# A load of batch 3's keys is issued ahead of a GpSimd wait in tile 1 of a pooled-attention and SiLU kernel

## The chip, the cores and the metric

The kernel runs on one core of a Trainium2 chip. The metric is the device time of one launch in microseconds (us); less is better. The core's engines are named as the profile names them: PE (TensorE, matrix products; PEld is its weight load), DVE (VectorE), ACT (ScalarE), POOL (GpSimd) and SP (SyncE, which here only issues DMAs). Each engine works through its own list of instructions in program order, and waits at an instruction until what that needs is there. A DMA is issued by an engine and then moves its data while that engine goes on.

## The reference

Attention with pooled keys and values, and behind it a two-layer network with SiLU:

```python
def _attn_ref(q, k, v):                       # q, k, v: 8 batches, 8 heads, 576 rows, 64 columns
    k_p = k.reshape(B, H, Sp, pool, D).mean(axis=3)     # pool = 8, so Sp = 72 keys are left
    v_p = v.reshape(B, H, Sp, pool, D).mean(axis=3)
    scores = scale * np.matmul(q, k_p.transpose(0, 1, 3, 2))
    scores = scores - np.max(scores, axis=-1, keepdims=True)
    attn = np.exp(scores)
    attn = attn / (np.sum(attn, axis=-1, keepdims=True) + 1e-09)
    return np.matmul(attn, v_p)

def _moe_ref(x, w_in, w_out):                 # x: 4608 x 512, w_in: 512 x 2048, w_out: 2048 x 512
    h = x @ w_in
    g = h * (1.0 / (1.0 + np.exp(-h)))
    return g @ w_out
```

The 8 batches of 576 rows, heads side by side, are the 4608 rows of x. All inputs and the output are float32.

## The kernel before

**Tiles and batches.** The 4608 tokens are done in nine tiles of 512 (the loop over `t`, `NT` = 9). A tile computes its two products with the weights, and beside them prepares the attention of the next tile, `a = t + 1`. As a batch has 576 tokens, tile `a` needs the pooled keys and values of batches up to `a`. So tile 1 finishes the keys of batch 2 and fetches those of batch 3, tile 2 finishes those of batch 3, and so on.

**The products.** Each product is done on blocks with seven multiplications instead of eight, which needs sums of blocks beforehand: of the weights (`weight_sum` L828 and `unit_weight_sum`, into w_sum and w_sum1), of x (`unit_x_sum` L715, into x_sum) and of the hidden layer (`hidden_sum` L817, into h_sum), all on DVE. The matrix products of the first layer are L874 (banks u_psA, u_psE, u_psB), those of the second L893 (o_psA, o_psE, o_psB). DVE's L908, L925 and L903 add or copy between these banks.

**Order.** A tile's products are a string of short names (`ORDER`, `FOUR`, for tile 1 `ONE`) which is walked step by step. All other work of the tile is a list of fillers: `at(s, fn, ...)` puts a call at step `s`. `spread` (L662) sorts them by step, keeps the order in which they were given within one step, and calls each when the products have come to its step. This sets the order of every engine's list of instructions by hand; the engines then wait for one another's results. Two fillers are there only for a wait: `behind_weight_sums` (L721) and `behind_x_sums` (L718) copy one element of the last weight sum, or the last x sum, into `gate` on POOL, so that what POOL has behind it starts only after DVE's sums.

**The keys of batch 3 and later.** `load_one` (L182, its DMA for keys is L189) loads the first four of each eight rows that are pooled, 576 KB, into a tile of its own tag. `load_rest` (its DMA is L221) loads the other four and adds them onto the first, in the DMA itself; it has to wait until the first has landed. `pool_k` adds up the four that are left on POOL (`pool_rows`, L227 and L230, into kp). `k_transpose` turns kp on PE (L292, at step 34 of the tile, into kT_ps) and copies it on ACT (L298, into kz); `spread_keys` (L279, at step 35, on DVE) makes kzr of it. The values of batch 3 go by `load_one` and `load_rest` too, in two DMAs each (`load_v_half`, L211). Batch 2's keys are loaded in another way, in slots, and summed by `slot_sums` (L346) on POOL; batch 2's values have the second half added by `load_v_half(2, 1)` and are summed by `pool_rows` on DVE at step 69 of tile 1.

**POOL's list at the start of tile 1.** The last filler of tile 0 on POOL is a `spread_keys` (L279). Then come, all at step 0, `behind_weight_sums` and the `slot_sums` of batch 2's keys (five sums and results in two groups); at step 1 the adding load of batch 2's values (two DMAs); at step 3 `load_one` for batch 3's keys, then for its values; at step 5 `load_rest` for both; at step 33 the load of batch 3's queries. In tile 2 POOL goes on with `behind_x_sums`, `pool_k` and `load_one` for batch 4's keys.

Of the kernel before, what the change touches and what calls it, by code (L numbers as in the profile page):

```python
# [36 lines left out]
def kernel(  # L37
# [156 lines left out]
    def last_rows(bs):  # L194

        lasts[bs] = mid.tile([128, 2, 2 * PH], FP32, tag="r_raw", bufs=1, name="r_raw")
        return lasts[bs][:, : len(bs)]
# [28 lines left out]
    def pool_rows(dst, raw, eng=nc.gpsimd):  # L226
        eng.tensor_add(  # L227
            out=raw[:, :, : 2 * D], in0=raw[:, :, : 2 * D], in1=raw[:, :, 2 * D :]
        )
        eng.tensor_add(out=dst, in0=raw[:, :, :D], in1=raw[:, :, D : 2 * D])  # L230
# [4 lines left out]
    def value_tile(b):  # L235
        vp = mid.tile([128, 4, D], BF16, tag="vp", name="vp")
        batches[b]["vp"] = vp
        return vp
# [927 lines left out]
    for t in range(NT):  # L1166
        a = t + 1
        if t == 0:
            f = []

            def at(s, fn, *args, **kw):
                f.append((s, lambda: fn(*args, **kw)))

            for n in (0, 2, 1, 3):
                at(0, unit_x_sum, 0, n)
            for y, y_at in ((2, 0), (3, 18), (1, 66)):
                for n in range(4):
                    at(y_at + n, unit_weight_sum, y, y + 1, n)
            for n in range(3):
                at((39, 42, 43)[n], slot_sums, "k", 0, levels=(n,))  # L1180
            at(45, slot_sums, "k", 1)
            for a in range(2):
                at(50, q_transpose, 1, a, 0, QI - UT)
            for j in range(2):
                at(55, select_k, 1, j)
            at(55, copy_k, 1, slice(0, 2), nc.scalar.copy)
            for i0, i1 in ((0, SA), (SA, SLOTS), (SLOTS, SLOTS + 1)):
                at(47, load_slots, nc.gpsimd, 2, "k", i0, i1)
            at(47, load_q, 2)
            for a in range(2):  # L1190
                at(55 + a, q_transpose, 1, a, QI - UT, UT)
            at(52, attn_tables)
            for i in range(PW):
                at(63 + i, weight_sum, 0, i)
            for n in (1, 2, 3):
                at(89, weight_sum, n, 0)
            at(93, weight_sum, 1, 1)
            for j in range(2):
                at(75 + j, slot_sums, "v", j)
                at(90, select_v, 1, j)  # L1200
            at(90, copy_v, 1, 0, nc.scalar.copy, H)
            at(92, turn_v, 1)
            at(84, load_first_values, 2)
            at(48, lambda: nc.gpsimd.memset(last_rows((1, 2))[:, :, :1], 0.0))
            at(80, load_v_last, 1, 2)
            at(84, spread_keys, 1, nc.gpsimd)
            at(60, scores_half, 1, 0)
            at(73, scores_half, 1, 1)
            for n in range(2):
                at(83, denominators, 1, n)  # L1210
                at(83, reciprocals, 1, n)
            at(95, numerators, 1, 0)
            at(95, numerators, 1, 1)
            for n in range(2):
                at(95, x_half, 1, n)
            at(96, moe_tables)
            tile_products(0, FIRST, f)
            continue

        order = ORDER.get(t, FOUR if t < NT - 1 else BARE)  # L1220
        if t == NT - 1:
            order = order.replace("P4 Q4", "R4 S4")
        o = 0
        f = []

        def at(s, fn, *args, **kw):
            f.append((s, lambda: fn(*args, **kw)))

        def late(s, fn, *args, **kw):
            at(s + o, fn, *args, **kw)  # L1230

        if t == 1:
            for n in (0, 2, 1, 3):
                at(0, unit_x_sum, 1, n)
            for n in (2, 3):
                at(0, weight_sum, n, 1)
            at(0, behind_weight_sums)
        late(43, hidden_sum, 2, 0, 4)
        late(53, hidden_sum, 2, 4, 8)
        late(64 if t < NT - 1 else 57, hidden_sum, 0, 0, 4)  # L1240
        late(64 if t < NT - 1 else 62, hidden_sum, 1, 0, 4)
        late(65, hidden_sum, 0, 4, 8)
        late(66, hidden_sum, 1, 4, 8)
        late(76, hidden_sum, 3, 0, 8)
        if a < B:
            if t == 1:
                for j in range(2):
                    at(0, slot_sums, "k", j, eng=nc.gpsimd)
                    at(46, select_k, 2, j)
                    at(47, copy_k, 2, j, nc.scalar.copy)  # L1250
                at(1, load_v_half, 2, 1)
                at(69, lambda: pool_rows(value_tile(2), batches[2]["v_raw"], nc.vector))
                at(50, spread_keys, 2)
                for n in "kv":
                    at(3, load_one, 3, n)
                at(44, last_sums, 1, 2, eng=nc.vector, levels=(0,))
                at(84, last_sums, 1, 2, eng=nc.vector, levels=(1, 2))
                at(46, load_v_last, 3)
                at(86, last_values, 1, 2, eng=nc.vector)
                for n in "kv":  # L1260
                    at(5, load_rest, 3, n)
                at(33, load_q, 3)
            else:
                at(0, behind_x_sums)
                at(0, pool_k, a)
                if a + 1 < B:
                    at(0, load_one, a + 1, "k")
                at(1, pool_v, a)
                if a + 1 < B:
                    at(1, load_one, a + 1, "v")  # L1270
                    at(1, load_v_last, a + 1)
                    at(3, load_rest, a + 1, "k")
                    at(4, load_rest, a + 1, "v")
                    at(33, load_q, a + 1)
                at(34, k_transpose, a)
                at(35, spread_keys, a)
        if t < NT - 1:
            tail = QI - UT + 2 * t
            for n in range(2):
                at((22, 32)[n], q_transpose, a, n, 0, tail)  # L1280
                if tail < UT:
                    at((47, 55)[n], q_transpose, a, n, tail, UT)
            late(63, attn_tables)
            late(63, scores, a)
            late(88, sums_and_values, a)
            late(89, x_part, a, 0)
            late(89, moe_tables)
            late(95, x_part, a, 1)
        if t < NT - 1:
            for n in (0, 2, 1, 3):  # L1290
                late(102 if (t, n) == (1, 0) else 105, unit_x_sum, t + 1, n)
        tile_products(t, order, f, last=t == NT - 1)
# [28 lines left out]
```

## Time and profile before

| | |
|---|---|
| median of 3 runs | 267.33 us (267.11 to 267.76) |
| profiled execution, its own time | 269.37 us |
| its span, first to last instruction | 267.7 us |
| mean granted PE clock | 1.000 |
| busy time PE / PEld | 260.7 us (97%) / 211.8 us (79%) |
| busy time DVE / ACT / POOL | 210.2 us (79%) / 182.3 us (68%) / 116.7 us (44%) |
| chain that ended last | PE 78%, DMA 11%, POOL 5%, DVE 4% |
| DMA raw<-in_k_dram in that chain | 8% |
| first layer's products of tiles 1, 2, 3 begin on PE | 47.19, 74.69, 103.76 us |

Busy time is the time in which an engine had an instruction under way; a busy PE is not PE at its peak. The chain is followed back from the last instruction, at each step to what released it. In a timeline each line is a start in us, a length in us, engine, line of the kernel, operation, what it writes and reads, shapes and how many; in brackets stands how long the engine was idle before it and what ended that. DMA share is the mean busy share of the core's 16 DMA engines; it can go a little over 1. A DMA's time to landing is counted from its issue.

### The profile page before, as it was taken

The page shows a single profiled execution, that of the slowest core. Times are in us where ns is not written, and L with a number is a line of the kernel's source. Part 1 is how long each engine was busy: PE and PEld are TensorE (multiplying, and loading weights), DVE is VectorE, ACT ScalarE, POOL GpSimd, SP SyncE. Part 2 cuts the span into 40 slices and gives each one's busy share as a digit, 9 for nine tenths or more (in the row PEclk, how much of TensorE's full clock was granted, in tenths as well). Part 3 has the DMA queues.
Part 4 walks back from the last instruction along what each step waited for, and adds up shares of the span by engine and source line. Part 5 has one row for each costly group of instructions (what it writes and reads, how often), then busy time and mean ns, then how long its engine had stood idle before and what let it go on. Part 6 is the DMA issues. An engine that isn't in the chain of part 4 may idle for free.

```text
span 267.7 us, 7702 instructions
## 1 busy us (share of the span) xinstructions
PE 260.7 (97%) x3136; PEld 211.8 (79%) x3136; DVE 210.2 (79%) x375; ACT 182.3 (68%) x319; POOL 116.7 (44%) x156
## 2 busy tenths in 40 slices
PE   8999999999997999999999999999999999999994
PEld 4468644888886788888888888888888887888883
DVE  3878879889886959895979598859886987687862
ACT  1489867888657865886587658765876677667700
POOL 8664774590609843853296229764900000000000
PEclk9999999999999999999999999999999999999999
DMA  7999999679598799679566956699400150015004
GB/s 191 283 205 272 223 283 290 176 167 195 123 177 209 193 162 190 152 178 175 121 164 153 191 113 151 154 169 140 117 2 0 40 119 3 2 32 127 2 0 157
DMA packets 31266, 38.84 MB, mean 145 GB/s; under 512 B 9776, under 2 KB 21488, under 8 KB 31232
## 3 DMA queue, kind: packets, MB, share of 16 engines
q0 software_dynamic: 22416, 25.84, 51.9%
q1 hardware_dynamic: 8384, 11.87, 16.5%
q10 hardware_dynamic: 432, 0.66, 1.1%
q8 instruction: 24, 0.39, 0.6%
q14 instruction: 10, 0.08, 0.1%
HBM read 37.75 MB, written 9.44 MB: 176 GB/s over the span
## 4 chain that ended last, share of the span: by engine, by line
PE 78%; DMA 11%; POOL 5%; DVE 4%; issue 1%; ACT 0%; POOLq 0%; DVEq 0%
PE o_psB L893 14%; PE u_psB L874 14%; PE o_psA L893 9%; PE o_psE L893 9%; PE u_psE L874 9%; PE u_psA L874 9%; DMA raw<-in_k_dram 8%; PE o_ps L792 4%; DMA raw<-in_v_dram 3%; PE hp_ps L764 3%; POOL raw L346 2%; PE sc_ps L555 1%; PE den_ps L584 1%; PE nu_ps L609 1%; POOL raw L227 1%; DVE raw L346 1%
## 5 line engine op out<-in xcount | busy, mean ns | idle before, releaser
L874 PEld LDWEIGHTS <-w_sum 128*128 128x128 bf16 x544 | 52.9, 98 | 6.9 <-issue 0.3
L893 PEld LDWEIGHTS <-h_sum 128*128 128x128 bf16 x512 | 48.9, 98 | 7.6 <-issue 0.4
L874 PEld LDWEIGHTS <-w_in_sb 128*128 128x128 bf16 x408 | 39.8, 98 | 4.9
L893 PEld LDWEIGHTS <-h_T 128*128 128x128 bf16 x384 | 37.0, 98 | 5.2 <-issue 0.4
L874 PE MATMUL u_psA<-xT,w_in_sb 128*128 128x256 bf16 x272 | 40.7, 273 | 0.0
L874 PE MATMUL u_psB<-x_sum,w_sum 128*128 128x256 bf16 x272 | 40.2, 273 | 0.1
L893 PE MATMUL o_psA<-w_out_sb,h_T 128*128 128x256 bf16 x256 | 32.0, 273 | 0.0
L893 PE MATMUL o_psB<-w_sum,h_sum 128*128 128x256 bf16 x256 | 31.8, 273 | 0.0
L908 DVE TENSOR_TENSOR u_psE<-u_psB,p 128x512 f32<-128x512 f32 x34 | 23.6, 697 | 9.1 <-PE u_psB L874 4.7
L912 ACT ACTIVATE h_T<-u_psE 128x512 bf16<-128x512 f32 x34 | 20.3, 597 | 10.6 <-PE u_psE L874 10.3
L925 DVE TENSOR_TENSOR c<-u_psB,p 128x512 f32<-128x512 f32 x34 | 23.2, 681 | 3.1 <-PE u_psB L874 2.1
L650 DVE TENSOR_TENSOR xT<-nu_ps,rec 128x512 bf16<-128x512 f32 x28 | 17.9, 682 | 9.4 <-ACT rec L634 9.4
L903 DVE COPY u_psB<-u_psA 128x512 f32<-128x512 f32 x30 | 20.9, 698 | 4.7 <-PE u_psA L874 4.2
L912 ACT ACTIVATE h_T<-u_psB 128x512 bf16<-128x512 f32 x34 | 20.4, 600 | 5.5 <-PE u_psB L874 5.5
L912 ACT ACTIVATE h_T<-u_psA 128x512 bf16<-128x512 f32 x34 | 20.4, 601 | 5.0 <-PE u_psA L874 5.0
L906 ACT COPY p<-u_psE 128x512 f32<-128x512 f32 x34 | 20.1, 596 | 4.0 <-PE u_psE L874 4.0
L211 POOL DMA_DIRECT2D v_raw<-in_v_dram x20 | 18.0, 992 | 11.0 <-DMA v_raw<-in_v_dram 11.0
L817 DVE TENSOR_TENSOR h_sum<-h_T 128x1024 bf16<-128x1024 bf16 x32 | 21.9, 687 | 0.2 <-ACT h_T L912 0.2
L912 ACT ACTIVATE h_T<-c 128x512 bf16<-128x512 f32 x34 | 21.7, 638 | 0.1
L817 DVE TENSOR_TENSOR h_sum<-h_T,h_sum 128x1024 bf16<-128x1024 bf16 (+1 forms) x24 | 20.7, 863 | 0.2
L874 PE MATMUL u_psB<-xT,w_sum 128*128 128x256 bf16 x136 | 20.4, 273 | 0.0
L874 PE MATMUL u_psE<-x_sum,w_in_sb 128*128 128x256 bf16 x136 | 20.4, 273 | 0.0
(127 smaller groups left out, 462.0 us busy)
## 6 DMA issues: line engine op xcount, KB each, us to landing
out_dram<-o_sb SPq DMA_DIRECT2D x128, 64.0 KB
raw<-in_k_dram POOLq DMA_DIRECT2D x10, 576.0 KB, 8.7
v_raw<-in_v_dram POOLq DMA_DIRECT2D x20, 256.0 KB, 6.0
q_bf<-in_q_dram POOLq DMA_DIRECT2D x5, 576.0 KB, 9.1
w_in_sb<-in_moe_w_in_dram POOLq DMA_DIRECT2D x8, 256.0 KB, 7.6
w_out_sb<-in_moe_w_out_dram POOLq DMA_DIRECT2D x8, 256.0 KB, 8.6
r_raw<-in_v_dram SPq DMA_DIRECT2D x28, 64.0 KB
raw<-in_v_dram POOLq DMA_DIRECT2D x2, 768.0 KB, 7.9
```

The lines of the kernel that those rows point to most:

```text
L211: nc.gpsimd.dma_start(out=batches[b]["v_raw"][KM * g : KM * (g + 1)], in_=source(b, "v")[:KM, 4 * g : 4 * (g + 1), PH * half : PH * (half ...
L346: eng.tensor_add(out=dst if w == D else raw[..., :w], in0=raw[..., :w], in1=raw[..., w : 2 * w],)
L650: nc.vector.tensor_mul(out=xT[:, 2 * g : 2 * g + 2, x_cols(t, f)], in0=st["nu"][g][f], in1=inv[:, f : f + 1, :].broadcast_to([128, 2, NQ]),)
L792: nc.tensor.matmul(ps["m", m], lhsT=h_T[:, g, m * 128 : (m + 1) * 128], rhs=w_out_sb[:, g, :], start=(g == 0), stop=(g == KG - 1),)
L817: nc.vector.tensor_tensor(out=h_sum[n][:, k0:k1, :], in0=get(a), in1=get(b), op=op)
L874: nc.tensor.matmul(ps[y, BANK[n]][:, u, :], lhsT=w[:, kk, 128 * u : 128 * (u + 1)], rhs=x[:, kk, :], start=n in (1, 5) and u == 0 and kk == 0,
L893: nc.tensor.matmul(o_bank(n, c), lhsT=left(n, kt, c), rhs=w[:, kt, :], start=n in (1, 5) and kt == 0 and c == 0, stop=kt == KQ - 1, skip_g ...
L903: (acopy if t == 0 or (t == 1 and y in (0, 1)) else vcopy)(ps[y, "B"], ps[y, "A"])
L906: acopy(f32[y], ps[y, "E"])
L908: tt(out=ps[y, "E"], in0=ps[y, "B"], in1=f32[y], op=add)
L912: nc.scalar.activation(h_T[:, g : g + 2, j * NQ : (j + 1) * NQ], src, func=AF.Silu)
L925: tt(out=c22, in0=ps[y, "B"], in1=f32[y], op=add)
```

## The change

In tile 1 `load_one(3, "k")`, the first of the two loads of batch 3's keys, moves from step 3 to step 0, and within step 0 ahead of `behind_weight_sums`. POOL so issues it before the copy that waits for DVE's weight sums, before the `slot_sums` of batch 2's keys and before the adding load of batch 2's values. The load itself, its tile, its size and its issuing engine are as before. `load_one(3, "v")` stays at step 3 and `load_rest` for both at step 5.

```diff
             for n in (2, 3):
                 at(0, weight_sum, n, 1)
+            at(0, load_one, 3, "k")
             at(0, behind_weight_sums)
...
                 at(1, load_v_half, 2, 1)
                 at(69, lambda: pool_rows(value_tile(2), batches[2]["v_raw"], nc.vector))
                 at(50, spread_keys, 2)
-                for n in "kv":
-                    at(3, load_one, 3, n)
+                at(3, load_one, 3, "v")
                 at(44, last_sums, 1, 2, eng=nc.vector, levels=(0,))
```

## The prediction

> **What bounds the kernel now.** I read the page first: PE is busy for 260.7 of 267.7 us, at a granted clock of 1.0 in all slices. A change away from PE can then only pay where PE stands still. So I read PE's waits next: after the head of the kernel there is one that counts, kT_ps L292 on GpSimd's kp L230, 1.4 us, once. The chain of the work that ended last tells where it comes from (columns: start us, length us, what):
>
> ```profile
> 49.58 0.19 POOL gate L721
> ...
> 55.88 1.30 POOL raw L211 x2
> 57.18 11.70 DMA raw<-in_k_dram
> 68.88 0.29 issue
> 69.17 10.88 DMA raw<-in_k_dram
> 80.05 0.07 issue
> 80.12 2.35 POOL raw L227
> ...
> 82.55 1.27 POOL kp L230
> ...
> 83.87 0.30 PE kT_ps L292 x4
> ```
>
> Read upwards: PE's transposition of batch 3's keys (83.87) waits for GpSimd's sums (80.12 to 83.82), these for the second, adding load (69.17 to 80.05), and that for the first load (57.18 to 68.88). The first load is late only because GpSimd stands ahead of it, in program order. GpSimd's own timeline shows what it stands at (start, length, idle time before in brackets):
>
> ```profile
> 44.01 0.41 POOL L279 TENSOR_TENSOR kzr<-kz,mask_k 128x128 bf16<-128x128 bf16 x1
> 49.58 0.19 POOL L721 COPY gate<-w_sum 128x1 bf16<-128x1 bf16 x1 [5.15 <-DVE w_sum L828]
> ...
> 75.65 0.19 POOL L718 COPY gate<-x_sum 128x1 bf16<-128x1 bf16 x1 [2.22 <-DVE x_sum L715]
> ```
>
> It idles 5.15 us before the gate, then sums batch 2's keys until 55.85 and issues two loads. Behind the late first load it idles 8.98 us again, at the second load.
>
> What PE loses I take by laying tile 2 beside tile 3, which has the same sequence with its keys in time (PE's timeline):
>
> ```profile
> 82.11 0.38 PE L874 MATMUL u_psB<-x_sum,w_sum 128*128 128x256 bf16 x2
> 83.87 0.30 PE L292 MATMUL kT_ps<-shifts,kp 128*128 128x72 bf16 x4 [1.38 <-POOL kp L230]
> ...
> 111.19 0.38 PE L874 MATMUL u_psB<-x_sum,w_sum 128*128 128x256 bf16 x2
> 111.40 0.29 PE L292 MATMUL kT_ps<-shifts,kp 128*128 128x72 bf16 x4
> ```
>
> From start to start it is 1.76 us in tile 2 and 0.21 in tile 3: 1.55 us lost. A second loss follows. VectorE's timeline has the spreading of these keys at
>
> ```profile
> 85.09 1.40 DVE L279 TENSOR_TENSOR kzr<-kz,mask_k 128x128 bf16<-128x128 bf16 x1
> ...
> 112.66 0.54 DVE L279 TENSOR_TENSOR kzr<-kz,mask_k 128x128 bf16<-128x128 bf16 x1
> ```
>
> In tile 2 it falls together with GpSimd's v_raw sum (L227, 85.04 to 86.33) and takes 1.40 instead of 0.54. The sum L908 behind it on VectorE comes late, and PE's next u_psB starts 0.74 us after u_psA (86.41 to 87.15), where tile 3 has 0.43 (113.94 to 114.37): 0.31 lost. Together 1.86. Check: from first u_psA to first u_psA tile 2 takes 29.07 (74.69 to 103.76), tile 3 27.10. Of the 1.97 between them 0.12 is other work (87.15 to 103.76 is 16.61, 114.37 to 130.86 is 16.49), which leaves 1.85.
>
> **The change, step by step.** It adds no instruction and takes none away. One DMA of 576 KB, L189, changes its place on GpSimd's queue, ahead of the gate, batch 2's sums and two loads of batch 2's values (L211).
>
> *The moved issue.* GpSimd is free at 44.42. A pattern in the idle times of its DMAs (at 43.37 the 41st issue waits for the 33rd to land) says that at most eight are under way, so this one waits for the 34th, q_bf at 36.25, which landed after 7.2 us, at 43.45: no wait. The two nearest issues of L189 took 1.72 (57.18) and 0.91 (84.11), so it ends by 46.2, and the gate still comes at 49.58: 0 us. Whether it slows VectorE's xT and x_sum, which run from 44.12 and feed PE at 47.19, no row shows at that place. The least is nothing, and no reason gives a gain. The most is a VectorE that stands still for 1.72 us: xT, done at 46.60, would be 1.1 us late for PE. I take 0, by the nearest row: two w_sum sums (L828, 42.70) took 1.28 us together, beside loads issued at 42.33 and 43.37, against 0.68 for one alone at 48.23.
>
> *Its transfer.* Ahead of it on GpSimd's queue batch 2's loads land at 50.1 (q_bf, 41.03 + 9.1) and 52.6 (raw, 43.37 + 9.2). DMA is full until 50 (share 1.03 to 1.15 from 44 to 49) and then has room: by slices of 1 us the share from 50 to 57 is 0.47, 0.29, 0.36, 0.48, 0.59, 0.66, 0.41, so 3.7 us of all engines are free. The load needs about 3.2 (an estimate: queue q0 holds 51.9% of 267.7 us for 25.84 MB, 5.4 us per MB, times 0.59 MB). Bounds for its landing: 50.7 (44.43 plus the 6.3 of the one at 84.11) and 59.5 (plus the 15.1 of the slowest load of the stage, q_bf at 71.34). I take 55.5, when the free share has added up.
>
> *What moves up behind it.* Batch 2's two adding loads stay at 55.88 and 56.50. Batch 3's values (L211) come at 57.2 instead of 58.08, and the second load of the keys at about 58.5 instead of 69.17. The 8.98 us stall goes; late next is the adding load of batch 3's values, which waits for their first half. The keys' second load now has the same bytes ahead of it that all landed by 69.3. Only a plain transfer has become an adding one, and these are slower: 113 GB/s at a share of 0.79 (73 to 74) against 196 at 1.19 (60 to 61). That is about 5.2 against 3.0 us for 0.59 MB, so it lands near 71.5. Bounds: 65 (58.5 + 7.2 of the adding load at 56.50, less than 1 us for its smaller size) and 80.2 (69.3 + 10.9), the last without any gain.
>
> *The end of it.* GpSimd's sums then wait for the gate at 75.65 instead of the data: L227 at 75.84, kp done at 79.55 (2.35 + 1.27 and 0.09 between). PE wants it at 82.3. So 2.8 us of cover remain, and the keys' data may land as late as 78.5 before PE stands. At 82.3 GpSimd stands as in tile 3, where kp is done 2.89 us before kT_ps. So kzr should take about 0.54 and the 0.31 go too. From tile 3 on the loads find their buffers without PE waiting, and the chain is PE to the end: what is won stays.
>
> Sum: 267.70 − 1.86 = 265.84 of span. The profiled execution's own time is 269.37, 1.67 above its span and 2.04 above the median of the runs, so it would become 267.51. From the median, **267.33 − 1.86 = 265.5 us**.
>
> **The rivals.**
> *Half the gain.* The wait goes, but kzr still meets a GpSimd sum (gain 1.55, 265.8), or the keys land between 78.5 and 80 (each us takes one; 1 us late gives 266.5). For: DMA is crowded from 58 to 69 (share 0.57 to 1.19). Against: 4 us of cover up to the gate.
> *Nothing.* The first load, though issued early, lands no earlier than the values behind it, and the second near 80: 267.3. Against: DMA's free room from 50 to 57.
> *Slower, by VectorE's queue.* At 64.53 VectorE sums batch 2's values (L227), whose adding loads landed at 59.9 and 63.7, 0.83 us before. Behind that sum stand h_sum and vr, and PE's weight load L621 waited 0.2 us for vr at 69.3. If the moved load is still under way at 55.9, these adding loads queue behind it. The first 0.83 of delay and 0.26 of idle time before 67.06 cost nothing; each us beyond costs PE one. At the upper bound for its landing (59.5) the delay is 3.6, the loss 2.5, the time 265.5 + 2.5 = 268.0; it is slower than before from a delay of 2.95. Against: landing at 55.5 gives no delay.
> *The issue held off by VectorE.* From 44.12 to 49.51 VectorE works without a gap. If GpSimd could not issue beside it, the load would go at 49.5, the gate and batch 2's sums slip by up to 1.72 to 57.57, against PE's select at 57.55, and the first load would end near 60, the second load still before 78.5: 265.5 to 266.5. Against: the two issues at 42.33 and 43.37 took 0.65 and 0.63 beside VectorE's sums. The Trainium skill, "SBUF — State Buffer", "Summary: rules for kernel authors", speaks for this rival: it warns against hiding a GpSimd-issued load beside a VectorE operation, since its descriptors starve while VectorE is in a 2x or 4x mode. The same page, "Who interferes with whom", gives tensor_tensor no two-port mode, and only such sums run here; by that, the trace agrees.
>
> **How the numbers follow.** The forecast has 0.72; its own range is 265.2 to 265.9 (gain 1.4 to 2.1). Half the gain 0.12, the issue held off 0.04, nothing 0.06, slower 0.06. A measurement of this kernel can tell about 0.3%, 0.8 us, from no change, so faster means below 266.5: 0.72, most of half the gain (0.09) and of the held-off issue (0.03), 0.84. Same: the rest of these and nothing, 0.10. Slower 0.06. Range 265.0 to 266.7: it reaches to a keys' landing 1 us late.
>
> **What would show it.** L189 at about 44.4, before the gate, which stays at 49.6. L221 at 58 to 60 with no long idle time. L227 at 75.8 behind the gate, not behind a DMA. kT_ps 0.21 us after the u_psB before it, kzr near 0.5, tile 2 at about 27.2 us. The prediction is wrong if L227 still names the DMA, if VectorE idles at 64.5, or if the gate moves.

## The result, and the profile after

The changed kernel takes 274.57 us (median of six runs, 273.67 to 276.64) against 267.56 (six runs, 267.11 to 269.25) for the kernel before, measured beside it: the ratio is 1.026, with a 95% interval from 1.021 to 1.031. It is slower by 7 us, where the prediction had it faster by 1.9. The profiled execution of the changed kernel took 273.67 us, its span is 271.9 at a granted clock of 0.998. In the experiments, executions that took over 1.5% more than the fastest of their kernel are left out of times and ratios: two of ten with the early extra load, one of four with two late ones, one of four with early and late ones, two of twelve in the last form of the loads held back.

I lay the steps of the forecast beside the trace first. GpSimd's timeline of the changed kernel (start, length, idle time before in brackets):

```profile
43.64 0.90 POOL L189 DMA_DIRECT2D raw<-in_k_dram  x1
49.42 0.18 POOL L721 COPY gate<-w_sum 128x1 bf16<-128x1 bf16 x1 [4.88 <-DVE w_sum L828]
...
58.73 1.92 POOL L221 DMA_DIRECT2D raw<-in_k_dram  x1
65.91 2.06 POOL L211 DMA_DIRECT2D v_raw<-in_v_dram  x2 [5.27 <-DMA v_raw<-in_v_dram]
...
81.95 0.19 POOL L718 COPY gate<-x_sum 128x1 bf16<-128x1 bf16 x1 [13.23 <-DVE x_sum L715]
82.10 2.34 POOL L227 TENSOR_TENSOR raw<-raw 72x1024 f32<-72x1024 f32 x1
```

The early load costs GpSimd nothing, the gate has not moved (49.42, before 49.58), the keys' second load goes out at 58.73 instead of 69.17 and, by the trace, lands at 71.60. The keys' sums then wait for the gate and no longer for a DMA. All this is as forecast. But the gate itself stands at 81.95, 6.3 us later than before (75.65). The chain of work that ended last, for the changed kernel and cut to the stretch in which that time is lost, says where it comes from:

```profile
44.00 14.67 DMA r_raw<-in_v_dram
58.67 0.02 issue
58.69 2.77 DMA out_dram<-o_sb
61.47 0.24 DVE r_raw L254
...
69.56 7.82 DMA out_dram<-o_sb
...
77.69 0.69 DVE o_sb L955
```

No keys are in it. It holds two kinds of transfers that the prediction never looked at, both on SP's queue: the loads of r_raw (eight of 64 KB, the last rows of the values of batches 1 and 2) and the stores of tile 0's output out of o_sb (sixteen of 64 KB). The engines that stand behind them are VectorE and, behind VectorE, PE. VectorE's timeline, first of the kernel before, then of the changed one, and PE's of the changed one:

```profile
58.60 0.68 DVE L254 TENSOR_TENSOR r_raw<-r_raw 128x512 f32<-128x512 f32 x1
...
71.39 0.69 DVE L955 TENSOR_TENSOR o_sb<-o_psB,p 128x512 f32<-128x512 f32 x1
```

```profile
61.47 0.69 DVE L254 TENSOR_TENSOR r_raw<-r_raw 128x512 f32<-128x512 f32 x1 [2.95 <-DMA out_dram<-o_sb]
...
77.69 0.69 DVE L955 TENSOR_TENSOR o_sb<-o_psB,p 128x512 f32<-128x512 f32 x1 [3.45 <-DMA r_raw<-in_v_dram]
```

```profile
63.27 0.60 PE L874 MATMUL u_psB<-xT,w_sum 128*128 128x256 bf16 x4 [2.12 <-DVE c L925]
...
78.43 1.91 PE L893 MATMUL o_psB<-w_sum,h_T 128*128 128x256 bf16 x16 [2.56 <-DVE o_sb L955]
```

The names in the brackets are crossed: L254 reads r_raw and waits for the last r_raw load, L955 writes o_sb and waits for tile 0's last store. SP's DMAs take eight semaphores in turn, and the profile puts the wait down to another DMA on the same one. What tells it is the landing of each DMA in the trace:

| | before | after |
|---|---|---|
| last r_raw load landed | 56.09 | 61.09 |
| L254 starts | 58.60, not idle | 61.47, after 2.95 idle |
| tile 0's last store landed | 70.41 | 77.38 |
| L955 starts | 71.39, not idle | 77.69, after 3.45 idle |

Where VectorE does wait, it starts 0.3 to 0.4 us after the landing, in these two rows and in the experiments alike. Before, 2.5 us lay between the landing of the loads and the row that reads them, and 1.0 us for the stores; less those 0.3 to 0.4 us, some 2.1 and 0.7 us were to spare. Two more executions of the kernel before have the loads at 55.38 and 55.64 and the stores at 70.23 and 70.06, so the landings of before are steady. From first u_psA to first u_psA tile 1 takes 27.49 us before and 33.16 after (5.67 lost), tile 2 29.08 and 27.85 (1.23 won), the rest is alike to 0.2: 4.3 of span. The profiled executions' own times differ by 4.3; the other 2.7 of the 7.0 us between the medians are their places among the runs, 269.37 being 1.81 above the median of before and 273.67 being 0.90 below that of after.

Why do SP's transfers land late? The DMA view by queue (packets, MB, share of the 16 DMA engines), q0 being GpSimd's queue and q1 SP's. First the kernel before, then the changed one, from 50 to 58 us:

```profile
q1 hardware_dynamic: 726, 0.94, 43.0%
q0 software_dynamic: 70, 0.14, 8.7%
```

```profile
q0 software_dynamic: 260, 0.68, 38.1%
q1 hardware_dynamic: 340, 0.43, 19.7%
```

The room in the DMA engines, into which the prediction put the early load, was the time in which SP's queue moved its data. In these eight us GpSimd's queue moves 0.54 MB more, and SP's 0.51 MB less. It isn't that the engines are full: both queues together take 51.7% of them before and 57.8% after. What keeps SP's bytes out all the same, the last experiment shows. There was a second such room, at the end of the stretch in which GpSimd idled for 8.98 us (60.19 to 69.17) and issued nothing. From 66 to 72 us, again before and then after:

```profile
q0 software_dynamic: 319, 0.45, 29.5%
q1 hardware_dynamic: 304, 0.44, 24.5%
```

```profile
q0 software_dynamic: 801, 0.79, 87.3%
q1 hardware_dynamic: 391, 0.53, 28.3%
```

Before, the last six stores were issued from 58.76 to 62.85 and all landed only from 68.16 to 70.41, as GpSimd's queue ran dry. After, the keys' second load and the values behind it, which moved up, fill this stretch too. SP's queue moves more in it than before, 0.53 instead of 0.44 MB, but it has more left to move and isn't done.

### The profile page after: what moved, and what is told of

Its sections match the earlier page's. It is cut to its first block, busy times and chain, and to the rows that moved or that the text cites. A ratio compares the mean times of both kernels' runs of the same rounds, so it can differ in the third digit from the quotient of the medians.

```text
span 271.9 us, 7695 instructions
## 1 busy us (share of the span) xinstructions
PE 260.2 (96%) x3131; PEld 211.3 (78%) x3136; DVE 209.1 (77%) x375; ACT 182.3 (67%) x319; POOL 115.2 (42%) x156
## 4 chain that ended last, share of the span: by engine, by line
PE 68%; DMA 21%; DVE 3%; ACT 2%; SPq 2%; issue 1%; POOL 1%; DVEq 0%; POOLq 0%
PE o_psB L893 14%; PE u_psB L874 14%; PE o_psA L893 9%; PE o_psE L893 9%; PE u_psA L874 9%; PE u_psE L874 9%; DMA raw<-in_v_dram 6%; DMA r_raw<-in_v_dram 5%; DMA w_out_sb<-in_moe_w_out_dram 4%; DMA out_dram<-o_sb 4%; DMA w_in_sb<-in_moe_w_in_dram 2%; PE sc_ps L555 1%; PE den_ps L584 1%; PE nu_ps L609 1%; SPq L204 1%
## 5 line engine op out<-in xcount | busy, mean ns | idle before, releaser
L908 DVE TENSOR_TENSOR u_psE<-u_psB,p 128x512 f32<-128x512 f32 x34 | 23.6, 697 | 8.4 <-ACT p L906 4.3
L903 DVE COPY u_psB<-u_psA 128x512 f32<-128x512 f32 x30 | 20.8, 698 | 4.7 <-PE u_psA L874 4.2
L211 POOL DMA_DIRECT2D v_raw<-in_v_dram x20 | 17.4, 932 | 14.8 <-DMA v_raw<-in_v_dram 14.8
```

The lines of the kernel that those rows point to most:

```text
L211: nc.gpsimd.dma_start(out=batches[b]["v_raw"][KM * g : KM * (g + 1)], in_=source(b, "v")[:KM, 4 * g : 4 * (g + 1), PH * half : PH * (half ...
L903: (acopy if t == 0 or (t == 1 and y in (0, 1)) else vcopy)(ps[y, "B"], ps[y, "A"])
L908: tt(out=ps[y, "E"], in0=ps[y, "B"], in1=f32[y], op=add)
```

## The experiments

**Theories.** *Two rooms*: the early load takes SP's first room, what moves up behind it takes the second, and the stores come too late for o_sb. Rivals: *place* (the issue of the load beside VectorE's sums does the harm), *order* (the kernel's own loads on GpSimd's queue, in their new order, hold one another up), and *first wait* (the 2.95 us at L254 alone, the rest follows from it). The text names lines by their numbers in the two kernels, also where an edit has moved them.

### The load behind the gate

```diff
-            at(0, load_one, 3, "k")
             at(0, behind_weight_sums)
+            at(0, load_one, 3, "k")
```

> The changed kernel with the first load of batch 3's keys directly behind the gate (about 49.6 us) instead of ahead of it (43.6), still ahead of the sums of batch 2's keys. Theory SHARE: while GpSimd's queue has data to move, SP's queue gets little of the DMA engines, so SP's eight r_raw loads (issued 41.2 to 46.0) crawl until GpSimd's queue runs dry; in the trace of before that is at about 52 us, with the change about 57. Issued at 49.6 the load is still in time to keep GpSimd's queue busy from 52 to 57, so the last r_raw load lands near 60.5 (61.1 in the changed kernel, 56.1 before), VectorE idles 2 to 3 us before L254, and the time stays 271 to 275 us. Rival PLACE: the harm is done by issuing ahead of the gate, beside VectorE's sums. Then the loss goes: 265 to 268 us, no idle time before L254.

274.97 us, ratio 1.0245 (1.0182 to 1.0308). The place beside VectorE's sums is not the harm. The last r_raw load lands at 58.95 here, L254 idles 0.99 only, the stores end at 77.35, and L955 idles 5.57. So the second wait grows where the first is short. A new thing came with it, in PE's timeline:

```profile
78.42 3.57 PE L893 MATMUL o_psB<-w_sum,h_T 128*128 128x256 bf16 x16 [4.68 <-DVE o_sb L955]
```

The same sixteen products took 1.91 in the changed kernel. The windows of this run show the granted clock (the column behind the five engines' busy times and counts):

```profile
76.00:78.00 2.00, 0.00 (x0) 0.00 (x0) 0.33 (x1) 0.00 (x0) 0.00 (x0) 0.64 0.51 152
78.00:80.00 2.00, 1.58 (x8) 1.12 (x8) 1.97 (x5) 0.00 (x0) 0.00 (x0) 0.50 0.03 12
80.00:82.00 2.00, 2.00 (x12) 1.34 (x10) 1.80 (x5) 0.00 (x0) 0.07 (x1) 0.50 0.17 39
```

In an idle time of 4.68 us PE's clock is halved, in the trace for 6.83 us: from 76.56, while PE still stands, to 83.38, 4.97 us after it went on. The Trainium skill, "TensorE: Matmul & The Clock Gate", "Part 1: The HAM clock gate (the "warmup" mystery)", has half the clock after an idle window of 3413 ns, until a busy one; in its lengths the trace agrees (6.83 is twice 3.41, and with 3.83 us of idle time another run below shows 3.41), but an idle time of 2.99 us, shorter than that window, brings 3.41 us too, in the kernel with two late loads below. The 2.56 us in the profiled execution of the changed kernel brought none, but five of its six runs have a mean clock of 0.988 or 0.994 (one stretch of 3.41 us takes 0.006 off such a mean), so its median carries it.

### Half of the load early

```diff
-            at(0, load_one, 3, "k")
+            at(0, load_one_part, 3, 0, 4)      # four of the eight heads
             at(0, behind_weight_sums)
...
+                at(3, load_one_part, 3, 4, 8)
                 at(3, load_one, 3, "v")
```

> The changed kernel with only half of the load (4 of 8 heads, 288 KB) ahead of the gate, the other half at its old place behind batch 2's adding loads. Theory SHARE: the delay of SP's r_raw loads goes by the bytes put ahead, so the last one lands near 58.6 instead of 61.1 (before: 56.1), VectorE's idle time before L254 falls from 2.95 to under 0.7 us, and SP's stores of tile 0 land near 73 to 74 instead of 77.4, which leaves a wait of 0 to 1.5 us at L955. 266 to 271 us. Rival PLACE or ORDER (any load there does it): 272 to 275 us.

267.39 us, 0.9976 (0.9948 to 1.0005). No wait at L254 or L955: r_raw lands at 59.60, and VectorE comes to L254 at 59.98, just in time (the head of this execution was longer; it is 11.4 us after the start of tile 1, as before). The stores end at 69.85, where I had expected 73 to 74. The second half of the keys, at its old place, holds the adding load back until 67.53, so most of the second room stays. Tile 2 takes 27.23, as tile 3 does. A gain can't be told from none here.

### Bytes alone, early, then late, then both

Three kernels leave all loads of the kernel before where they are and add loads of 512 KB that nobody reads: one early, at the place of the moved load; one late, at 59 us; two late. A fourth has the early one and the two late ones.

```diff
+            at(0, load_extra, 3)          # early: into h_sum, still unused then
             at(0, behind_weight_sums)
...
+                at(5, load_extra, 3)      # late: one or two, into tiles of tile 0
                 for n in "kv":
                     at(5, load_rest, 3, n)
```

> The kernel before, in its old order, with an extra load of 512 KB that nobody uses (rows of batch 3's keys in pieces of 1 KB, into space of h_sum that is written later) issued by GpSimd ahead of the gate; it does more work than needed. Theory SHARE: the extra bytes alone delay SP: last r_raw load near 60.5, VectorE idle 2 to 3 us before L254, SP's stores of tile 0 late too, so L955 waits 1 to 4 us; kT_ps L292 may still wait for kp. 270 to 275 us. Rival ORDER: the harm comes from what moved up behind the load, the adding loads issued at 58.7 and 65.9 instead of 69.2 and 70.1; these stay here, so 267 to 268.5 us.

> The kernel before, in its old order, with an extra load of 512 KB that nobody uses, issued by GpSimd at about 60 us, where it has issued batch 3's first loads and stands waiting for them; into the buffer of batch 2's keys, which is free by then. Theory STORES: bytes on GpSimd's queue between 60 and 71 us keep SP's stores of tile 0 back, wherever they come from. The last store lands at 73 to 76 us (70.4 before), L955 waits 1.5 to 4 us, tile 1 lasts 29 to 31.5 us (27.5 before); the adding load of the keys is late too, so kT_ps may wait longer. 269.5 to 274 us. Rival MOVED LOADS (only the order of batch 3's own loads matters, not the bytes): tile 1 stays at 27.5, 267 to 268.5 us.

> The kernel before with two extra loads of 512 KB that nobody uses, issued by GpSimd at about 59 to 60 us (twice the bytes of g3). Theory TWO ROOMS: the second room (66 to 72 us) is taken, the first (51 to 57) is not; ten of the sixteen stores go in the first, the other six wait behind the extra bytes and land near 71 to 73 us: L955 waits 0 to 1.5 us, tile 1 27.5 to 29 us. The keys' adding load is late behind the extra bytes, so kT_ps may wait 1 to 3 us: 267.5 to 271 us. Rival BYTES (1 MB late is enough by itself): L955 waits 3 us or more, tile 1 over 30.5 us.

> The kernel before, its own loads in the old order, with an extra 512 KB load ahead of the gate (as in e3) and two of 512 KB at about 60 us (as in h2). Theory TWO ROOMS: both rooms are taken, the stores land at 74 to 78 us, L955 waits 3 to 6 us, PE with it, perhaps with a halved clock behind it; tile 1 lasts 30.5 to 35 us: 271 to 277 us. Rival ORDER (only the moved adding loads of batch 3 do it): L955 waits under 1.5 us, tile 1 under 29.5 us, 267.5 to 270.5 us.

| added | time, ratio (interval) | last r_raw, last store | idle at L254 / L955 |
|---|---|---|---|
| early | 268.75, 1.0021 (0.9987 to 1.0055) | 58.40, 72.23 | 0.28 / 0.33 |
| one late | 267.69, 1.0005 (0.9970 to 1.0039) | 55.77, 70.31 | 0 / 0 |
| two late | 272.01, 1.0140 (1.0106 to 1.0174) | 55.29, 71.54 | 0 / 0.56 |
| early and two late | 272.99, 1.0214 (1.0169 to 1.0259) | 58.21, 75.57 | 0.53 / 2.66 |

Half a megabyte in either room does no harm that can be measured; for the early one I had expected 270 to 275 and for one late 269.5 to 274, and both fell. Two late came above the 267.5 to 271 that I had given them. A megabyte late costs 1.4%, but by another way than the stores: batch 3's own keys land later, PE waits 2.99 us for kp, and a stretch at a lower clock follows (0.63 from 86 to 90). Bytes in both rooms, half a megabyte early and a whole one late, give 2.1 of the 2.6 per cent, and here it is the stores: the last lands at 75.57, 4.0 us later than with the two late ones alone. VectorE waits 2.66 us at the sum into o_sb (L955 of the kernel before), ScalarE 4.26 at its copy into the other half (L938); PE stands 1.72 and 1.67 us behind these, and not for kp. VectorE's timeline of this kernel, in which the extra lines have moved the numbers:

```profile
58.58 0.69 DVE L273 TENSOR_TENSOR r_raw<-r_raw 128x512 f32<-128x512 f32 x1 [0.53 <-DMA out_dram<-o_sb]
...
75.88 0.69 DVE L974 TENSOR_TENSOR o_sb<-o_psB,p 128x512 f32<-128x512 f32 x1 [2.66 <-DMA out_dram<-o_sb]
```

With no load of the kernel moved in the order, *order* falls as the cause; bytes in SP's two rooms are enough.

### VectorE's sums of r_raw later

```diff
-                at(44, last_sums, 1, 2, eng=nc.vector, levels=(0,))
+                at(76, last_sums, 1, 2, eng=nc.vector, levels=(0,))
```

> The changed kernel with VectorE's first sum over r_raw (L254, the first level of last_sums for batches 1 and 2) at step 76 of tile 1 instead of 44, so that VectorE no longer stands at 58.5 us for the r_raw loads. Theory SHARE with two waits in a row: the idle time of 2.95 us before L254 goes, PE runs on from 61 to about 73, but SP's stores of tile 0 land by the DMA's clock, near 75 to 77, so VectorE waits longer for o_sb at L955 (3.45 us before, 4 to 6 now) and little is won: 271.5 to 275 us. Rival ONE WAIT: the wait for r_raw is the whole loss and the store wait only follows from it; then 266 to 269 us.

272.96 us, 1.0177 (1.0126 to 1.0228). L254 no longer idles, but L955 now idles 4.72 and PE 3.83; 1.1 us after PE went on, 3.41 us at half clock follow. The first wait had only used up a part of the second in advance. *First wait* falls.

### Other buffers for tile 1's output

```diff
+    def o_of(t):
+        return [row_tiles["k"][0][:, :2], row_tiles["k"][1]] if t == 1 else o_sb
...
-                    tt(out=o_sb[1][:, :, HI], in0=ps["o", "B"], in1=f32["o"], op=add)
+                    tt(out=o_of(t)[1][:, :, HI], in0=ps["o", "B"], in1=f32["o"], op=add)
```

(and so for the other copies and stores of tile 1). L955 then need not wait for tile 0's stores. The edit was made in the changed kernel, there also together with the later sums, and in the kernel before.

> The changed kernel, but tile 1 puts its outputs into the buffers of batch 2's keys (row_tiles k, free after their sums at 55.2 us) instead of o_sb, so that it need not wait until tile 0's stores have left o_sb. Theory STORES: the main loss is the wait for tile 0's stores (landed 77.4 us instead of 70.4), because the adding loads of batch 3, moved up to 58.7 to 67.2, keep GpSimd's queue full where SP's queue had its room. Then the wait at L955 goes whole, the wait of kT_ps for kp stays away, and what is left is VectorE's wait for r_raw at 58.6 (0 to 3 us): 265.5 to 268.5 us. Rival RRAW: the delay starts at r_raw and goes through VectorE's queue; another buffer for the outputs then changes little: 271 to 275 us.

> The last one and VectorE's first sum over r_raw at step 76 instead of 44: both waits are taken out by their causes. Theory STORES: nothing is left but the prediction's gain of 1.4 to 2.1 us against the kernel before: 265.2 to 266.2 us. Rival: a third wait takes their place (on vp, kz or the next tile's loads): over 267 us, and PE's waits name it.

> The kernel before, with tile 1's outputs in the buffers of batch 2's keys and nothing else changed. Theory STORES: before, tile 0's stores land at 70.4 us and L955 is due at 71.4, so the other buffers bring nothing: 266.8 to 268 us, kT_ps still waits 1.4 us for kp. Rival BUFFERS: the buffers are a gain by themselves, whatever the load does: under 266.5 us.

269.10 us, 1.0051 (1.0017 to 1.0086) for the first; 268.24, 1.0012 (0.9981 to 1.0043) with the later sums; 268.41, 1.0019 (0.9989 to 1.0050) for the kernel before. In the first the last store still lands late, at 77.07, but nobody stands behind it: tile 1 is back at 27.50 and tile 2 at 27.23. So the wait for o_sb is the main loss, 2.1 of the 2.6 per cent. All three came out above what I had given them (up to 268.5, 266.2 and 268). Of that, 0.3 us lies at the end: from the first u_psA of the last tile these three kernels take 28.58 us instead of 28.27. In the second, PE also stands 0.83 us for VectorE's L908, by the later sums. What else keeps the median of the first 0.5% up, with a profiled span of 266.5 in which PE stands nowhere for over 0.15 us from tile 1 on, I did not find.

### What moves up, held back

```diff
+    def behind_last_values():              # a copy on POOL that waits for VectorE's vr
+        nc.gpsimd.tensor_copy(out=gate, in_=batches[2]["vr"][:, 1, 3, 31:])
...
-                for n in "kv":
-                    at(5, load_rest, 3, n)
-                at(33, load_q, 3)
+                at(87, behind_last_values)
+                for n in "kv":
+                    at(87, load_rest, 3, n)
+                at(87, load_q, 3)
```

In this form all adding loads of batch 3 and its queries wait until 69.7; in the second form the keys' adding load stays up (at 58) and only the values and queries are held; the third is the second with the sums of r_raw at step 76.

> The changed kernel with o_sb as it was, but what comes behind on GpSimd (the adding loads of batch 3's keys and values, and its queries) is held back by a copy that waits for VectorE's vr, as late as in the kernel before or later (about 69 to 72 us); the first load of the keys stays early. Theory STORES: SP's queue has its room again between 60 and 70, the stores land near 70 to 73 and L955 waits 0 to 1 us; left are the wait for r_raw (0 to 3 us) and perhaps a little at kT_ps, since the keys' adding load lands near 79 to 81: 266.5 to 270.5 us. Rival EARLY LOAD: the early first load alone delays the stores past 75 us: 272 to 275 us.

> The changed kernel, with the adding load of batch 3's keys left where the change brings it (about 58.7 us), but the adding load of the values and the queries (1.1 MB) held back by a copy that waits for VectorE's vr (about 69 to 71 us). Theory STORES: up to 70 us GpSimd's queue then carries as many bytes as in the kernel before, the stores land near 70 to 72.5, L955 waits 0 to 1 us, kT_ps waits for nothing, and what is left is VectorE's wait for r_raw (0 to 3 us): tile 1 27.5 to 29.5, tile 2 27.2, 266.8 to 269.5 us. Rival KEYS ALONE: the keys' adding load at 58.7 is what keeps the stores back; L955 still waits 3 us or more, 271 to 275 us.

> g4 (early load, the keys' adding load moved up, values and queries held until VectorE's vr) with VectorE's first sum over r_raw at step 76 instead of 44, so that it does not wait for r_raw at 58.6 us. All waits found so far should be gone: tile 1 27.5, tile 2 27.2 us. Against an ordinary execution of the kernel before (tile 2 at 28.1) that is 0.9 us won: ratio 0.995 to 0.999. Rival: the stores (L955) or r_raw at its new place still wait 0.5 us or more, and the ratio is 1.000 to 1.006.

270.00 us, 1.0077 (1.0043 to 1.0112); 268.55, 1.0055 (1.0016 to 1.0094); 268.29, 1.0017 (0.9987 to 1.0046). With the second room given back, the last store lands at 67.48, 71.14 and 69.99, and L955 doesn't wait in any of them. What is left of the loss in the first two is the first room: L254 idles 0.83 and 0.95, and tile 1 takes 28.32 and 28.45 instead of 27.49; in the first form the held keys come late as well (PE waits 1.45 for kp). The third form has neither wait and tile 2 at 27.23, and is still no faster than the kernel before, where I had expected a ratio of 0.995 to 0.999.

### The kernel before, twice more

> The kernel before, unchanged, for a second profile. The prediction's 1.86 us came from one execution that took 269.37 us, 2.04 more than the median of 267.33. Theory RARE STALL: the wait of kT_ps for kp is short or absent in an ordinary execution of some 267.3 us, so tile 2 lasts 27.2 to 28.0 us here and the wait is under 0.8. Rival STEADY STALL: the wait of 1.4 us is always there, tile 2 lasts 29.1, and the execution of 269.37 was long for another reason.

> The kernel before, unchanged, for a third profile. As for the second: RARE STALL has tile 2 at 27.2 to 28.0 us where the time is about 267.3, and near 29 only where it is about 269; STEADY STALL has 29.1 in all.

267.91 and 268.04 us, spans 266.2 and 266.3. PE's timeline of the first:

```profile
82.40 0.30 PE L292 MATMUL kT_ps<-shifts,kp 128*128 128x72 bf16 x4 [0.38 <-POOL kp L230]
```

The wait that the prediction set out to remove is 0.38 and 0.52 us in these executions, not 1.38, and tile 2 takes 28.08 and 28.22 instead of 29.08 (I had expected up to 28.0). So about 0.85 to 1.0 us over 27.23 was there to be won, not 1.86. In the kernel with one late extra load, whose own loads stand in the old order, the wait did not come at all and tile 2 took 27.23.

### Tile 0's stores on two queues

```diff
-            store(0, m, slice(0, d_model))
+            store(0, m, slice(0, d_model), (nc.sync, nc.scalar))
```

> The changed kernel with tile 0's sixteen stores issued in turn by SP and by ScalarE, eight each, so that half of them need not wait for SP's places and have a queue of their own. Theory SP NARROW: the lateness comes from SP's queue, with its eight DMAs under way and its small share beside GpSimd's; with two queues the stores land near 69 to 73 us, L955 waits 0 to 1.5 us, tile 1 lasts 27.5 to 30 us: 266.5 to 270.5 us. Rival ENGINES FULL: the DMA engines as a whole are the limit, two queues change nothing, 272 to 276 us. ScalarE's own issues may cost it some tenths.

290.04 us, 1.0844 (1.0803 to 1.0886): missed by 20 us. ScalarE's timeline, with the issues as ACTq, shows why:

```profile
47.26 0.59 ACT L799 COPY o_sb<-o_ps 128x512 f32<-128x512 f32 x1 [1.60 <-PE o_ps L792]
56.55 2.80 ACTq L753 DMA_DIRECT2D out_dram<-o_sb  x2
59.39 0.59 ACT L799 COPY o_sb<-o_ps 128x512 f32<-128x512 f32 x1 [11.54 <-DMA r_raw<-in_v_dram]
```

The eight semaphores, the places of the DMAs under way, are shared by SP's and ScalarE's DMAs. ScalarE's first store went out only when the third r_raw load had landed (56.48, issued 56.55), the next of SP's when the fourth had (58.54, issued 58.60), and so on in turn; ScalarE's own copies stood behind its issues, and PE waited 19.4 us for its copy into u_psB (L903, which at the start of tile 1 is ScalarE's). The stores couldn't be parted from the r_raw loads in this way.

### Stores ahead of the r_raw loads

What was still open: do the stores land late because the r_raw loads hold the eight places, or because SP's queue gets too few bytes through? In these two the sixteen stores go first, the r_raw loads behind them, and L254 stands at step 76; once in the changed kernel, once in the kernel before.

```diff
-            at(80, load_v_last, 1, 2)          # tile 0
...
+            at(0, load_v_last, 1, 2)           # tile 1
...
-                at(44, last_sums, 1, 2, eng=nc.vector, levels=(0,))
+                at(76, last_sums, 1, 2, eng=nc.vector, levels=(0,))
```

> The changed kernel with SP's order turned round: the eight r_raw loads of tile 1 go behind tile 0's sixteen stores instead of ahead of them, and VectorE's first sums of r_raw (L254) stand at step 76 instead of 44 (about 66.4 us). All bytes stay. What is open: whether the stores land late because the r_raw loads hold all of SP's eight places while they crawl, or because SP's queue gets too few bytes through. Places: the stores go out from 47, land before 66, the loads go out from about 52 behind them and land before 66.4 too; neither L955 nor L254 waits, 266.5 to 268. Bytes: SP's 1.5 MB take until 73 to 77 in whatever order, now the loads come last; L955 no longer waits, but L254 stands 3 to 8 us, and PE with it at the products with vr (L621 and L609), 270 to 276.

> The kernel before with the same two edits (stores ahead of the r_raw loads on SP, first sums of r_raw at step 76), the early load not moved. Bytes: SP's queue has its first room from 51 to 57 here, so the stores land by about 62, but the last r_raw only in the second room, by 68 to 70.5; L254 stands 0 to 3.5 us, 267 to 270.5. Places: all landed by 62, no wait, 267 to 268, with the wait for kp (L292) as before, 0.4 to 1.4 us.

279.24 us, 1.0425 (1.0388 to 1.0463), and 276.52, 1.0321 (1.0284 to 1.0358). Both are slower still than I had given them, as the wait goes over to r_raw. VectorE's timeline, first of the changed kernel in this form, then of the one before:

```profile
76.29 0.69 DVE L254 TENSOR_TENSOR r_raw<-r_raw 128x512 f32<-128x512 f32 x1 [8.83 <-DMA r_raw<-in_v_dram]
```

```profile
72.31 0.69 DVE L254 TENSOR_TENSOR r_raw<-r_raw 128x512 f32<-128x512 f32 x1 [5.19 <-DMA r_raw<-in_v_dram]
```

The stores are not late in this order: the last lands at 60.71 and 56.31. The DMA view of the changed kernel in this form, from 50 to 58 us:

```profile
q1 hardware_dynamic: 670, 0.91, 40.3%
q0 software_dynamic: 203, 0.54, 32.2%
```

SP's queue moves 0.91 MB here beside 0.54 of GpSimd's, nearly as much as in the kernel before beside 0.14. So the first room has space for both. With the loads first, the stores wait behind the r_raw loads, which land late beside GpSimd's loads and hold the eight places until then; put behind the stores, the r_raw loads are slow in the next stretch (issued from 57.64, the last landed at 75.97). The last of these 24 transfers of SP's lands at 75.97 and 72.00 in these two, at 77.38 and 70.41 in the two kernels with the loads first. Neither answer is right alone: the order decides who is late, and the early load when SP's queue is done, 4.0 us later in the one order and 7.0 in the other.

## Why the prediction was wrong

*The moved issue* was right: 0.90 us, no harm to VectorE, the gate behind the weight sums stays. *Its landing* was forecast for 55.5 and came at 58.44, inside the bounds; the second load's for 71.5 came at 71.60; the sums wait for the gate; kT_ps doesn't wait; kzr takes 0.28. Tile 2 is 27.85 instead of 27.2, with 0.46 of it a wait for VectorE's copy L903 at the tile's start. So each step about the keys held, but for the time at which the gate behind the x sums comes (81.95, not 75.65), which is where the loss shows.

**The step that failed is "Its transfer"**: "DMA is full until 50 … and then has room … 3.7 us of all engines are free." The load did find its room, but what its transfer does to the others stands in the sum at nothing, without a reason. The share was added up and never split by queue: 0.94 of the 1.08 MB that moved from 50 to 58 were SP's, and who waits for them, with how much to spare (2.5 us from landing to use for r_raw, 1.0 for o_sb), was not asked. The runs show 5.0 us more for the last r_raw load (56.09 to 61.09), 7.0 for the last store, and 5.67 us lost in tile 1. The same step failed once more under "What moves up behind it": "The 8.98 us stall goes", and the only thing late next was sought on GpSimd's queue. At the end of that stall (69.17) SP's last six stores landed, from 68.16 to 70.41. The experiments with added bytes show that half a megabyte in either room costs nothing that can be measured, and that bytes in both do. Why the r_raw loads are so slow beside GpSimd's stays open in part (last section).

*The rival "Slower, by VectorE's queue"* named the engine and the sort of wait, not the transfer: it followed batch 2's adding loads to L227, which in the changed kernel starts without idle time (67.40). It gave 268.0 for a delay of 3.6 us. The real waits stood at L254 and L955, two rows of the same engine's list.

*The signs* for a wrong prediction (L227 names the DMA, VectorE idles at 64.5, the gate moves) did not show. They covered the steps that had been thought of. One of the signs for a right one was missing: L227 on GpSimd at 75.8 came at 82.10.

*A term was mis-sized*: 1.86 us came from one profiled execution that was 2.04 over the median, and the sum took it from the median. In two more executions 0.85 to 1.0 us were to be had. Without any harm by the transfer the forecast would so have been 266.3 to 266.5, not 265.5; the half-load kernel (0.9976) and the kernel with both waits removed (1.0017) don't show even that for certain.

## What to carry to other kernels

Room in the DMA share is not free before it is split by queue: name whose transfers use it, which of them stand at the head of that queue and hold back the others, who waits for these, and the slack from the landing to the wait. An idle stretch of the issuing engine can be what the other queue lives on, so ask of a stall that you remove which transfers landed in it. Take the size of a stall from more than one execution when the profiled one lies above the median.

## What the runs showed of the hardware that was new to me

- *A queue's share beside another.* From 46 to 50 us of the kernel before, the r_raw loads moved 0.11 MB while GpSimd's queue moved 0.85. With no bytes on GpSimd's queue (52.8 to 56.1) they land 0.54 to 0.76 us apart; in the changed kernel, beside GpSimd's loads, the first five land 2.4 us apart on average (49.10 to 58.67). The last three land 0.7 to 0.9 us apart although GpSimd's adding loads are under way by then, so the pace isn't one figure. They raise their semaphore in five steps, the stores in sixteen. The Trainium skill, "DMA: Bandwidth & Descriptors", "Why a DMA increments its semaphore by 16 and not by 1", has a DMA from SP use only as many DMA engines as divide the slowest dimension of both sides, with one step for each and one at once for the others: four heads, four engines, five steps; the trace agrees. An eighth of the bytes (half of 4 in 16) is an estimate if, as the same page's "Queues, rings and completion order" has it, an engine takes packets from its queues in turn, and if these are of one size; 0.11 of 0.96 MB is near it. The stores, with all sixteen engines, got 0.27 of 1.47 MB from 58 to 66 us, far from half, so that rule alone doesn't give their pace.
- *Eight under way.* In these kernels SP's and ScalarE's DMAs together have eight semaphores, in turn: the ninth issue waits for the first to land, whatever it is (before, r_raw loads land at 52.76 and 53.52, and stores go out at 52.82 and 53.53).
- *Half clock.* With idle times of PE of 2.99 and 3.83 us came 3.41 us at half the granted clock, with 4.68 and 6.11 us twice that, with 9.68 three times and with 19.41 six times. The stretch began 2.5 to 4.9 us after PE had come to stand, so mostly while it still stood (in the changed kernel with the stores first the clock is at 0.50 from 72 to 76 us, with PE idle), and ended 3.1 to 5.2 us after it went on.
